# Adding the decay terms of the early attention pairs on TensorE instead of fetching them as tiles

## The chip, the cores and the metric

One core of a Trainium2 chip runs the whole program once. The metric is device microseconds (us) of one execution: 717.03 us, the median of three runs (717.02 to 718.77).

## What is computed

Causal attention with a decay, then two expert layers, all in float32 (cut from the reference):

```python
# q, k, v: (2, 8, 576, 64); s: (2, 8, 576)
scores = q @ k.T / 8
cum = cumsum(maximum(s, 0))
scores = where(causal, -1e9, scores + minimum(-(cum[i] - cum[j]), 0))
attn = softmax(scores); out = attn @ v                 # -> x: (1152, 512)
x = sum_e p[e] * (maximum(x @ w1[e], 0) @ w2[e])       # 4 experts, F = 1024
y = (silu(x @ w_gate) * (x @ w_val)) @ w_out           # F = 1536
```

Softmax does not see a term that is the same along a row, so the kernel adds only the running sums of the keys ("decays") to the scores, a row vector that is the same for all queries of a head.

## The kernel before

**Attention.** Heads are taken in pairs (two heads of 64 dimensions share the 128 partitions). `pairs` (L349) lists sixteen: eight "early" ones for queries 0 to 255 (`pi < EXACT`), then eight "late" ones for queries 256 to 575. For each early pair and each of its two lanes (heads), `group` (L506) makes two score blocks, 128 x 128 and 128 x 256: `scores` (L519) multiplies keys and queries in float32 (L527) and adds a triangular mask by two small fp32r matmuls per block (`tri` times `idr`, L530). `least` (L532) on DVE adds the decays and finds the row extreme (L544, a tensor_tensor_reduce written as a custom instruction and a read of its accumulator). ACT takes the exponential and its sum (`exp`, L553), DVE inverts the sum (`guard`, L559 and L560), ACT or POOL scales the row (`norm`: L335 on ACT, L337 on POOL), PE transposes (`turn`, L598), ACT or DVE copies (`copy`, L327 on ACT, L329 on DVE), and PE multiplies by the values (`products`, L657). `values` splits the result into a high and a low fp32r part, `xh` and `xl`.

**The decays before.** `scan` and `center` turn `s` (16 rows) into `sums`. Each pair needs its two rows spread over all 128 partitions. For pairs 0 and 1 (`NSEL`) PE does it by a one-column selection (`pick`, L461) and ACT copies the result to a `dqe` tile. For pairs 2 to 7 `sums` is written to DRAM (`rows_e`) and fetched six times as a broadcast `dqe` tile, 256 KB each (the last `fetch` of `prepare`). Queries and keys of four pairs are fetched ahead (`NKQ`), the others when an earlier pair is under way.

**The experts.** `into` (L992 to L994, tile `wah`, plain) and `seven` (L1092 to L1094, tiles `wah`/`wsh`, a seven-product form of 2 x 2 blocks) make the hidden rows `hh` and `hl`, `outof` (L1154 to L1156) multiplies back into `acc`. Every product is three fp32r matmuls. Weights come as `raw` tiles (512 KB) and are split into high and low parts by POOL (L331, L340) during attention. Plain units of the first 512 tokens fill PE during attention; how many there are depends on when the plan sees attention end.

**What sets the order.** Every instruction stream is written by `Plan`: tasks have an engine, a cost from a table, a rank and dependencies; `step` takes the task that can start earliest by the plan's own clock, and the lower rank of two. The plan's clock decides the order only; on the chip each engine and each DMA queue runs its stream in order and waits on semaphores. While PE would be idle by the plan's clock, `fill` puts in transposes of the identity (`keep_on`, L409).

Of the kernel before, what the change touches and what calls it, by code (L numbers as in the profile page):

```python
# [17 lines left out]
P = 128  # L18
# [5 lines left out]
NS = 5  # L24
NKQ = 4
NKP = 2
NBE = 3
NBL = 2
NSEL = 2
# [40 lines left out]
CUM2 = 10  # L70
CUMAT = 14.0
FIX2 = 8
HOLDW = 8.0
# [14 lines left out]
    "scale": {"v": (0.063, 0.00104), "a": (0.1, 0.00084), "p": (0.243, 0.00084)},  # L88
# [6 lines left out]
def f32(ap):  # L95
    return ap.bitcast(F32)
# [42 lines left out]
class Task:  # L139
# [141 lines left out]
def attention_moe_swiglu(ctx, tc, q_early, q_late, k, v, s, dp, w1, w2, wg, wv, wo, out):  # L281
# [69 lines left out]
    def attention(ap, ps):  # L351
        BH = B * H
        one = ap.tile([P, S], F32, name="one", tag="ns", bufs=NS)[:BH, :]
        sr = ap.tile([P, NB - 1, 320], F32, name="sr", tag="p", bufs=NPT).rearrange("p c t -> p (c t)")[:BH, :S]
        ncum = ap.tile([P, S], F32, name="ncum", bufs=1)[:BH]
        sums = ap.tile([P, S], F32, name="sums", bufs=1)[:BH]
        early, later, whole = slice(0, 2 * P), slice(2 * P, S), slice(0, S)
        rows_e, rows_l = (scratch.tile([BH, n], F32, name=f"rows{n}", bufs=1) for n in (2 * P, S))
# [3 lines left out]
        mask = ap.tile([P, P], F32, name="mask", bufs=1)  # L362
# [7 lines left out]
        t_sr = fetch(lambda: sr, s, 36, [], -100, take=[ring("p", NPT)])  # L370
# [3 lines left out]
        def upper():  # L374
            nc.gpsimd.memset(mask, 0.0)
            nc.gpsimd.affine_select(
                out=mask, in_=mask, pattern=[[-1, P]], compare_op=ALU.is_ge, fill=-2.0 ** 103, base=0, channel_multiplier=1)
        t_up = add("pool", 0.6, upper, [t_id], rank=-98)
        lo, hi = half
        t_clear = [any_of("v", "fill", 2 * P, lambda e: nc.vector.memset(f32(idr).rearrange("p o n -> p (o n)"), 0.0), [], rank=-97),  # L380
                   any_of("v", "fill", D, lambda e: nc.vector.memset(f32(tri[hi, hi]), -2.0 ** 103), [], rank=-97)]
        spread = [(idr[lo, 0, :], ident[lo, :]), (idr[hi, 0, lo], ident[hi, hi]), (idr[lo, 1, hi], ident[lo, lo]), (idr[hi, 1, :], ident[hi, :])]
        spread2 = [(tri[lo, 0:P], mask[lo, :]), (tri[hi, lo], mask[hi, hi]), (tri[lo, P:], mask[lo, lo]), (tri[hi, P:], mask[hi, hi])]
        t_mask = [any_of("av", "copy", P, lambda e, x=x: move(e, *x), t_clear + [t], rank=-96.5)
                  for y, t in ((spread, t_id), (spread2, t_up)) for x in y]

# [11 lines left out]
        t_scan = add("dve", dve(2 * P), lambda: scan(early), [t, t_one], rank=-98)  # L398
        t_early = add("dve", dve(2 * P), lambda: center(early, P - 1), [t_scan], rank=-98)
        t_rows = [fetch(lambda: rows_e, sums[:, early], 16, [t_early], -97.5)]  # L400
        t = any_of("p", "fill", S - 2 * P, lambda e: positive(e, later), [t_sr], rank=CUM2)
        t_scan2 = add("dve", dve(S - 2 * P), lambda: scan(later), [t, t_scan], give=[(t_sr, ring("p")), (t_one, ring("ns"))], rank=CUM2)

# [11 lines left out]
        def load(quad, deps):  # L415
# [8 lines left out]
            t = fetch(to, v[b, hp // 2, :, :kb], kb * 128, deps, -50 + 10 * quad if quad < 2 else starts[2 * quad] - LOADS,  # L424
# [6 lines left out]
        def prepare(pi, release):  # L431
# [15 lines left out]
            if not exact and pi == EXACT:  # L447
                t_mid = add("dve", dve(S), lambda: center(whole, 3 * P + P // 4 - 1), [t_scan2, t_early] + t_rows, rank=CUM2)
                t_rows.append(fetch(lambda: rows_l, sums, 36, [t_mid], CUM2))
            w = 2 * P if exact else BANK  # L450

            def bias():
                decay[pi] = ap.tile([P, 2, w], F32, name="d" + tag, tag="d" + tag, bufs=NBE if exact else NBL)
                return decay[pi]
            rg = ring("d" + tag, NBE if exact else NBL)
            if pi < NSEL:
                def pick():
                    bias()
                    tp = ps.tile([P, BANK], F32, name="tp", tag="tp", bufs=2)
                    for j in range(2):  # L460
                        nc.tensor.matmul(tp[:, j * w:j * w + w], ident[:BH, BP * j + m:BP * j + m + 1].to_broadcast([BH, P]),  # L461
                                         sums[:, early], start=True, stop=True)
                    decay[pi, "tp"] = tp
                first = add("pe", 2 * pe32(w), pick, [t_early, t_id, chain_d.get(tag)], mode="s", take=[rg, ring("tp")], rank=rank)
                tb = [any_of("a", "bank", 2 * w, lambda e: move(e, decay[pi].rearrange("p j n -> p (j n)"), decay[pi, "tp"]), [first],
                             give=[(first, ring("tp"))], rank=rank - 60)]
            else:
                of = rows_e if exact else rows_l
                first = fetch(bias, lambda: of[m::BP, :w].partition_broadcast(P), 2 * w // 2, [release, t_rows[-1], chain_d.get(tag)], rank + 0.2, take=[rg])
                tb = [first]  # L470
            chain_d[tag] = first
            used[pi] = [(tq, ring(tag)), (first, rg)]
            if not exact:
                def both(j):
                    def to():
                        if j == 0:
# [1111 lines left out]
```

## Time and profile before

| | |
|---|---|
| median of 3 runs | 717.03 us |
| the profiled execution: its own time / its span | 719.07 us / 717.2 us |
| PE, matmul busy | 698.9 us, 97% |
| DVE / ACT / POOL busy | 557.2 / 358.2 / 463.2 us |
| first dense matmul (L992) | 35.97 us |
| last product of attention (L657) starts | 132.06 us |

The profile is of one execution. A matmul's row is longer than the time until the next matmul starts, since they are pipelined; the distance of two starts is what one costs in a row of them. "Idle before <-" at the end of a row is how long the engine stood still before it and what the profile thinks ended the wait. L numbers are lines of the kernel before.

### The profile page before, as it was taken

To read this page: it belongs to the slowest core of one execution; us is meant where nothing else is said; L and a number is where in the kernel's file an instruction comes from. 1 tells how busy PE (TensorE), PEld (TensorE's weight loads), DVE (VectorE), ACT (ScalarE), POOL (GpSimd) and SP (SyncE) were. 2 spreads that over 40 slices of the span, in tenths; PEclk is the share of its full clock that TensorE was granted. 3 is DMA by queue.
4 is the path that set the end of the run, shared out by engine and by line. 5 is a ranking of instruction groups with operands and counts; after the bars stand their busy time and mean duration, and the time that the engine had idled before them with its cause. 6 is when DMAs were issued, how large, how long until landed. Compare 5 with 4: busy or idle time off the path is not lost.

```text
span 717.2 us, 11928 instructions
## 1 busy us (share of the span) xinstructions
PE 698.9 (97%) x4280; PEld 607.2 (85%) x4280; DVE 557.2 (78%) x1081; ACT 358.2 (50%) x757; POOL 463.2 (65%) x436
## 2 busy tenths in 40 slices
PE   8899999999999999999999999999999999999997
PEld 6676666787898989898989888997989999999996
DVE  5686575797278899999999999766884777787665
ACT  5787777423444545555565654655644424233210
POOL 3743242599366667666767678799899868585321
PEclk9999999999999999999999999999999999999999
DMA  8794642112204445465446553222121202010003
GB/s 206 241 306 125 205 135 85 31 58 71 106 0 148 147 157 168 147 207 166 147 160 194 188 186 103 65 86 89 39 80 31 82 23 74 30 31 1 1 1 133
DMA packets 31452, 79.80 MB, mean 111 GB/s; under 512 B 3568, under 2 KB 9216, under 8 KB 31392
## 3 DMA queue, kind: packets, MB, share of 16 engines
q1 hardware_dynamic: 31248, 78.90, 34.4%
q8 instruction: 34, 0.56, 0.3%
q14 instruction: 26, 0.21, 0.1%
q10 hardware_dynamic: 144, 0.13, 0.1%
HBM read 67.16 MB, written 11.85 MB: 110 GB/s over the span
## 4 chain that ended last, share of the span: by engine, by line
PE 74%; DVE 12%; POOL 5%; issue 4%; ACT 4%; DMA 0%; DVEq 0%; ACTq 0%; POOLq 0%
PE h L1092 10%; PE h L1094 10%; PE h L1093 10%; PE o L1154 10%; PE o L1155 10%; PE o L1156 10%; PE tp L598 2%; PE po L657 2%; PE sp L527 2%; DVE tt L1031 1%; ACT ns L553 1%; PE h L992 1%; DVE cc L1111 1%; PE h L994 1%; PE h L993 1%
## 5 line engine op out<-in xcount | busy, mean ns | idle before, releaser
L1111 DVE TENSOR_TENSOR cc<-cc,h 128x320 f32<-128x320 f32 (+1 forms) x282 | 124.9, 452 | 49.3 <-PE h L1094 43.0
L1154 PE MATMUL o<-woh,hh 128*128 128x512 f32 x396 | 157.3, 397 | 2.9 <-DVE acc_a L1242 1.6
L1156 PE MATMUL o<-woh,hl 128*128 128x512 f32 x396 | 154.7, 391 | 1.7 <-DVE hl L340 1.7
L1155 PE MATMUL o<-wol,hh 128*128 128x512 f32 x396 | 155.8, 393 | 0.0
L1092 PE MATMUL h<-xh,wsh 128*128 128x320 f32 (+1 forms) x312 | 92.9, 298 | 0.0
L1094 PE MATMUL h<-xh,wsl 128*128 128x320 f32 (+1 forms) x312 | 92.8, 297 | 0.0
L1093 PE MATMUL h<-xl,wsh 128*128 128x320 f32 (+1 forms) x312 | 92.7, 297 | 0.0
L340 POOL TENSOR_TENSOR wal<-raw,wah 128x512 fp32r<-128x512 f32 (+1 forms) x58 | 70.8, 1230 | 32.4 <-ACT wah L327 31.4
L1156 PEld LDWEIGHTS o<-woh,hl 128*128 128x128 f32 x396 | 74.4, 188 | 18.6 <-DVE hl L340 2.1
L340 POOL TENSOR_TENSOR wol<-raw,woh 128x512 fp32r<-128x512 f32 x54 | 79.2, 1475 | 15.0 <-ACT woh L327 14.5
L1154 PEld LDWEIGHTS o<-woh,hh 128*128 128x128 f32 x396 | 74.5, 188 | 16.6 <-DVE acc_a L1242 2.3
L1155 PEld LDWEIGHTS o<-wol,hh 128*128 128x128 f32 x396 | 74.5, 188 | 10.8
L1211 ACT ACTIVATE cc<-cc 128x640 f32<-128x640 f32 (+1 forms) x46 | 32.1, 698 | 91.7 <-DVE cc L1111 91.6
L340 POOL TENSOR_TENSOR hl<-cc,hh 128x512 fp32r<-128x512 f32 (+1 forms) x28 | 41.9, 1498 | 52.8 <-ACT hh L1214 52.6
L1092 PE MATMUL h<-xh,wah 128*128 128x320 f32 (+1 forms) x234 | 69.4, 297 | 0.0
L1094 PE MATMUL h<-xh,wal 128*128 128x320 f32 (+1 forms) x234 | 69.4, 296 | 0.0
L1093 PE MATMUL h<-xl,wah 128*128 128x320 f32 (+1 forms) x234 | 69.3, 296 | 0.0
L340 POOL TENSOR_TENSOR wsl<-sf,wsh 128x512 fp32r<-128x512 f32 x44 | 66.8, 1537 | 0.8 <-ACT wsh L327 0.8
L1242 DVE SCALAR_TENSOR_TENSOR acc_b<-o,pr,acc_b 128x512 f32<-128x512 f32 x75 | 55.5, 743 | 8.4 <-PE o L1156 8.1
L1092 PEld LDWEIGHTS h<-xh,wsh 128*128 128x128 f32 x312 | 58.9, 189 | 1.5
L1093 PEld LDWEIGHTS h<-xl,wsh 128*128 128x128 f32 x312 | 59.0, 189 | 1.4
L1094 PEld LDWEIGHTS h<-xh,wsl 128*128 128x128 f32 x312 | 59.0, 189 | 0.0
(146 smaller groups left out, 1667.8 us busy)
## 6 DMA issues: line engine op xcount, KB each, us to landing
raw<-in_w SPq DMA_DIRECT2D x42, 512.0 KB, 5.0
n<-hl SPq DMA_DIRECT2D x36, 256.0 KB, 2.3
raw<-n SPq DMA_DIRECT2D x18, 512.0 KB, 3.3
hh<-in_wg SPq DMA_DIRECT2D x12, 512.0 KB, 4.2
hh<-in_wv SPq DMA_DIRECT2D x12, 512.0 KB, 4.0
hh<-in_wo SPq DMA_DIRECT2D x12, 512.0 KB, 3.9
dql<-rows SPq DMA_DIRECT2D x8, 512.0 KB, 5.1
vr<-in_v SPq DMA_DIRECT2D x4, 640.0 KB, 4.4
```

The costliest lines, as they stand in the source:

```text
L340: {"v": nc.vector, "p": nc.gpsimd}[e].tensor_tensor(to, x, f32(y), op=ALU.subtract)
L527: nc.tensor.matmul(sp[j][:, at:at + w], Q[half[j], x], K[half[j], :w], start=True, stop=False)
L598: nc.tensor.transpose(tp[:kn, x * P:x * P + P], box["ns"][lane][:, at + c * P:at + c * P + kn], ident)
L1092: nc.tensor.matmul(hp, wh, h, start=c == 0, stop=False)
L1093: nc.tensor.matmul(hp, wh, l, start=False, stop=False)
L1094: nc.tensor.matmul(hp, wl, h, start=False, stop=c == 1)
L1111: nc.vector.tensor_tensor(part(k), part(x), banks[i], op=ALU.add)
L1154: nc.tensor.matmul(op, hh[:, f, ts], wh[:, f, :], start=f == 0, stop=False)
L1155: nc.tensor.matmul(op, hh[:, f, ts], wl[:, f, :], start=False, stop=False)
L1156: nc.tensor.matmul(op, hl[:, f, ts], wh[:, f, :], start=False, stop=f == NF - 1)
L1211: nc.scalar.activation(src()[:, o], src()[:, o], AF.Relu)
L1242: nc.vector.scalar_tensor_tensor(acc(t), bank_(), sc, acc(t), op0=ALU.mult, op1=ALU.add)
```

## The change

The decays of all early pairs are added on PE. `sums` is split into a high part `sh` and the negative of what is left, `sb` (two DVE instructions, `split`). The sixteen rows of `s` are laid out by the host in four blocks of 32 partitions, so that each half of 64 partitions holds high and low parts of every head; `sel` is a one-hot column with a minus sign. `decays` adds `sel` times `sb` into the open accumulation of the score bank: four fp32r matmuls of 64 rows per pair. The mask becomes a constant second operand of `least`, 128 x 256, instead of eight `tri` matmuls per pair. `pick`, the `dqe` tiles, `rows_e` and its fetches fall away for the early pairs. Queries and keys of all eight early pairs are fetched at once (`NKQ` 8), the first 256 columns of `s` ahead of the other 320. Plan: first weight load not before 16 instead of 8 (`HOLDW`), some costs and ranks are other numbers, a link on the same engine costs nothing. Late pairs keep their `tri` matmuls and fetched decays.

```diff
-NKQ = 4
+NKQ = 8
-CUM2 = 10
+CUM2 = 18
-HOLDW = 8.0
+HOLDW = 16.0
-    "scale": {"v": (0.063, 0.00104), "a": (0.1, 0.00084), "p": (0.243, 0.00084)},
+    "scale": {"v": (0.063, 0.00104), "a": (0.19, 0.00084), "p": (0.243, 0.00084)},
...
-                d.end + (LINK[d.eng] if d.eng != "pe" or e != "pe" else 0.0) if d.eng != "dma" or e != "dma" else 0.0))
+                d.end + (LINK[d.eng] if d.eng != e else 0.0) if d.eng != "dma" or e != "dma" else 0.0))
...
-        t_sr = fetch(lambda: sr, s, 36, [], -100, take=[ring("p", NPT)])
+        t_sr = fetch(lambda: sr[:, early], s[:, early], 128, [], -100, take=[ring("p", NPT)])
+        t_sr2 = fetch(lambda: sr[:, later], s[:, later], 160, [t_sr], -56)
...
+        t = add("dve", 0.22, lambda: nc.vector.reduce_sum(one_hot, ident.rearrange("p (q i) -> p i q", i=32), axis=AX.X), [t_id], rank=-98)
+        t_sel = add("dve", 0.12, lambda: nc.vector.tensor_scalar(sel, one_hot, -1.0, 1.0, op0=ALU.mult, op1=ALU.mult), [t], rank=-98)
...
-        t_rows = [fetch(lambda: rows_e, sums[:, early], 16, [t_early], -97.5)]
+        def split():
+            nc.vector.tensor_copy(sh, sums[:, early])
+            nc.vector.scalar_tensor_tensor(sb, f32(sh), low_rows[:, 0:1], sums[:, early], op0=ALU.mult, op1=ALU.subtract)
+        t_early = add("dve", 0.75, split, [t, t_low], rank=-98)
...
+            if exact:
+                used[pi] = [(tq, ring(tag))]
+                t_ready[pi] = [tk, tq, t_early, t_sel], [t_up]
+                return
...
+                if pi < EXACT:
+                    for qb, at, w in segs:
+                        for j in range(2):
+                            nc.tensor.matmul(sp[j][:, at:at + w], Q[half[j], qb * P:qb * P + P], K[half[j], :w], start=not at, stop=False, skip_group_check=True)
+                    if pi:
+                        decays()
+                    return
...
+            def decays():
+                for qb, at, w in segs:
+                    for j in range(2):
+                        nc.tensor.matmul(box["sp"][j][:, at:at + w], sel[half[j], BP * j + m:BP * j + m + 1].to_broadcast([D, P]), sb[half[j], :w],
+                                         start=False, stop=True, skip_group_check=True)
...
-                        todo = [(at, at + w, box["sp"][lane][:, at:at + w], decay[pi][:, lane, :w])]
+                        todo = [(at, at + w, box["sp"][lane][:, at:at + w], mask[:, 2 * P - w:] if pi < EXACT else decay[pi][:, lane, :w])]
```

What it moves, in the order of the streams. PE, at the first two pairs (`o<-ident` are fillers, `sp` and `h` the score banks, `tp<-sums` the selection). Before:

```order
L409 MATMUL o<-ident 128x128 x18
L527 MATMUL sp<-k_106,qe 128x128 x2
L530 MATMUL sp<-tri,idr 128x128 x2
L530 MATMUL sp<-tri,idr 128x64 x2
L527 MATMUL sp<-k_106,qe 128x256 x2
L530 MATMUL sp<-tri,idr 128x128 x2
L530 MATMUL sp<-tri,idr 128x64 x2
L461 MATMUL tp<-sums,ident 128x256 x4
L527 MATMUL h<-k_107,qe 128x128 x2
```

With the change:

```order
L425 MATMUL o<-ident 128x128 x18
L533 MATMUL sp<-k_109,qe 128x128 x2
L533 MATMUL sp<-k_109,qe 128x256 x2
L425 MATMUL o<-ident 128x128 x3
L548 MATMUL sp<-sb,sel 128x128 x2
L548 MATMUL sp<-sb,sel 128x256 x2
L533 MATMUL h<-k_110,qe 128x128 x2
```

Eight mask matmuls and the selection (for two pairs at once) have gone, four decay matmuls stand in each pair.

SP, the DMA queue, from the fourth transfer on (`dqe` and `rows_104` are the decays, `raw` the weights, `vr` values). Before:

```order
L368 DMA rows_104<-sums 16x256
L368 DMA qe<-in_q_early 128x256
L368 DMA vr<-in_v 128x512 x2
L368 DMA k_110<-in_k 128x256
L368 DMA dqe<-rows_104 128x2x256
L368 DMA rows_105<-sums 16x576
L368 DMA k_111<-in_k 128x256
L795 DMA raw<-in_w 128x1024
L368 DMA dqe<-rows_104 128x2x256
L368 DMA qe<-in_q_early 128x256
L795 DMA raw<-in_w 128x1024
```

With the change, the rows from the last queries on:

```order
L369 DMA k_116<-in_k 128x256
L369 DMA qe<-in_q_early 128x256
L369 DMA rows<-sums 16x576
L369 DMA vr<-in_v 128x512
L818 DMA raw<-in_w 128x1024 x3
L369 DMA vr<-in_v 128x512
L369 DMA k_109<-in_k 128x320
```

All early queries and keys are now ahead of the first weights, no `dqe` transfer is left, and the weights stand behind a `vr` load that waits for the second pair's products to free its buffer.

POOL, from its first scaling (`ns`) on; `wah`/`wal` and `woh`/`wol` are the split weights. Before:

```order
L337 TENSOR_SCALAR ns<-ns,st 128x256
L337 TENSOR_SCALAR ns<-ns,st 128x128
L337 TENSOR_SCALAR ns<-ns,st 128x256 x2
L331 TENSOR_SCALAR wah<-raw 128x512
L337 TENSOR_SCALAR ns<-ns,st 128x128
L340 TENSOR_TENSOR wal<-raw,wah 128x512
```

With the change:

```order
L335 TENSOR_SCALAR ns<-ns,st 128x256 x2
L335 TENSOR_SCALAR ns<-ns,st 128x128 x2
L335 TENSOR_SCALAR ns<-ns,st 128x256
L329 TENSOR_SCALAR wah<-raw 128x512
L338 TENSOR_TENSOR wal<-raw,wah 128x512
L329 TENSOR_SCALAR wah<-raw 128x512
L335 TENSOR_SCALAR ns<-ns,st 128x128
L338 TENSOR_TENSOR wal<-raw,wah 128x512
```

Fourteen scalings now stand ahead of the first weight instead of four (only the last five are shown), and in the whole program POOL has eleven scalings of 128 x 128 instead of three, ACT five instead of thirteen. In the whole program there are also 35 fillers instead of 50, and one plain unit of 512 tokens (24 matmuls of 512 columns) is done in the seven-product form (42 of 256 columns), with one reload of a pair of weight tiles less.

## Rows read from the trace of the kernel before

**Rows 1.** Busy time by stretch: length, PE, PEld, DVE, ACT, POOL; clock, DMA share, GB/s.

```profile
9.37:35.97 26.60, 22.31 (x212) 17.74 (x209) 17.58 (x91) 21.29 (x80) 17.27 (x25) 1.00 0.84 233
62.33:134.40 72.07, 71.10 (x461) 47.19 (x460) 45.56 (x151) 51.18 (x123) 20.81 (x28) 1.00 0.39 125
400.00:500.00 100.00, 97.45 (x556) 86.91 (x555) 81.85 (x128) 56.46 (x107) 80.12 (x72) 1.00 0.38 124
500.00:600.00 100.00, 97.41 (x629) 90.99 (x630) 72.22 (x132) 42.95 (x89) 85.64 (x83) 1.00 0.17 54
```

**Rows 2.** Timeline, PE: dense matmuls of 256 and of 512 columns.

```profile
35.97 0.36 PE L992 MATMUL h<-xh,wah 128*128 128x256 f32 x1
36.17 0.28 PE L993 MATMUL h<-xl,wah 128*128 128x256 f32 x1
36.29 0.28 PE L994 MATMUL h<-xh,wal 128*128 128x256 f32 x1
...
73.94 0.39 PE L993 MATMUL h<-xl,wah 128*128 128x512 f32 x1
74.17 0.40 PE L994 MATMUL h<-xh,wal 128*128 128x512 f32 x1
```

**Rows 3.** Timeline, PE: fillers, first score group, selection.

```profile
1.65 3.79 PE L409 MATMUL o<-ident 128*128 128x128 f32 x18 [1.65 <-POOL ident masks.py:199]
5.37 0.49 PE L527 MATMUL sp<-k,qe 64*128 64x128 f32 x4
...
6.59 1.99 PE L461 MATMUL tp<-sums,ident 16*128 16x256 f32 x8
```

**Rows 4.** Timeline, DVE and ACT: running sums, first decays added, first exponential.

```profile
2.85 0.28 DVE L388 TENSOR_SCALAR sr<-sr 16x256 f32<-16x256 f32 x1 [0.30 <-DMA sr<-in_s]
...
4.34 0.86 DVE L391 TENSOR_TENSOR_SCAN ncum<-one,ncum,sr 16x320 f32<-16x320 f32 x1
...
9.06 0.27 DVE L544 CUSTOM_DVE_ANT_0 ns<-sp,dqe 128x128 f32<-128x128 f32 x1
...
9.37 0.40 ACT L553 ACTIVATE ns<-ns,st 128x128 f32<-128x128 f32 x1 [0.17 <-DVE st L544]
```

**Rows 5.** Timeline, ACT: three scalings and the idle time before them.

```profile
14.84 0.40 ACT L335 ACTIVATE ns<-ns,st 128x128 f32<-128x128 f32 x1 [1.14 <-DVE st L560]
...
20.19 0.40 ACT L335 ACTIVATE ns<-ns,st 128x128 f32<-128x128 f32 x1 [0.88 <-DVE st L560]
...
23.97 0.40 ACT L335 ACTIVATE ns<-ns,st 128x128 f32<-128x128 f32 x1 [1.73 <-DVE st L560]
```

**Rows 6.** Timeline, DVE and SP: decays added, and one issue of a decay transfer.

```profile
13.77 0.58 SPq L368 DMA_DIRECT2D dqe<-rows  x1
...
13.82 0.29 DVE L544 CUSTOM_DVE_ANT_0 ns<-sp,dqe 128x128 f32<-128x128 f32 x1 [1.34 <-PE h L527]
...
17.95 0.29 DVE L544 CUSTOM_DVE_ANT_0 ns<-h,dqe 128x128 f32<-128x128 f32 x1 [1.19 <-DMA dqe<-rows]
...
22.29 0.29 DVE L544 CUSTOM_DVE_ANT_0 ns<-sp,dqe 128x128 f32<-128x128 f32 x1 [2.19 <-POOL wal L340]
```

**Rows 7.** Groups by line and shape, ACT and POOL, 9.3 to 36 us.

```profile
L327 ACT COPY p<-tp 128x384 f32<-128x384 f32 x9 | 4.2, 461 | 0.2 <-PE tp L598 0.2
L335 ACT ACTIVATE ns<-ns,st 128x128 f32<-128x128 f32 x10 | 4.0, 401 | 5.1 <-DVE st L560 5.0
L335 ACT ACTIVATE ns<-ns,st 128x256 f32<-128x256 f32 x4 | 2.0, 504 | 0.0
...
L337 POOL TENSOR_SCALAR ns<-ns,st 128x128 f32<-128x128 f32 x3 | 1.1, 373 | 2.3 <-DVE st L560 1.3 <-ACT ns L553 1.0
```

**Rows 8.** DMA issues of the whole run: count, KB each, median us to landing.

```profile
raw<-in_w SPq DMA_DIRECT2D x42, 512.0 KB, 5.0
```

**Rows 9.** Timeline, POOL and DVE: a weight's low part beside a guard.

```profile
24.52 1.27 POOL L340 TENSOR_TENSOR wol<-raw,woh 128x512 fp32r<-128x512 f32 x1
...
24.89 0.92 DVE L559 TENSOR_SCALAR st<-st 128x2 f32<-128x2 f32 x1 [0.43 <-ACT ns L553]
```

More of the change, by code (lines that the diff above doesn't have):

```diff
@@ L24 @@
 NS = 5
-NKQ = 4
+NKQ = 8
 NKP = 2
-NBE = 3
 NBL = 2
-NSEL = 2
 NPT = 4
@@ L452, in bias @@
+            if pi == EXACT:
+                t_mid = add("dve", dve(S), lambda: center(whole, 3 * P + P // 4 - 1), [t_scan2, t_early], rank=CUM2)
+                t_rows.append(fetch(lambda: rows_l, sums[:BH], 36, [t_mid], CUM2))
             def bias():
-                decay[pi] = ap.tile([P, 2, w], F32, name="d" + tag, tag="d" + tag, bufs=NBE if exact else NBL)
+                decay[pi] = ap.tile([P, 2, BANK], F32, name="dql", tag="dql", bufs=NBL)
                 return decay[pi]
-            rg = ring("d" + tag, NBE if exact else NBL)
@@ L456, in prepare @@
[L456 to L470, printed above, removed]
+            rg = ring("dql", NBL)
@@ L471, in prepare, with both, to @@
+            first = fetch(bias, lambda: rows_l[m::BP, :BANK].partition_broadcast(P), BANK, [release, t_rows[-1], chain_d.get(tag)], rank + 0.2, take=[rg])
+            tb = [first]
             chain_d[tag] = first
             used[pi] = [(tq, ring(tag)), (first, rg)]
[L473 to L476, printed above, removed]
-                            decay[pi, 2] = ap.tile([P, S], F32, name="d2", tag="d2", bufs=NBL)
-                        return decay[pi, 2][half[j]]
-                    return to
-                t2 = []
-                for j in range(2):
-                    t2.append(fetch(both(j), lambda j=j: rows_l[BP * j + m, :].partition_broadcast(D), 144, [release, t_rows[-1]] + t2,
-                                    rank + 0.3, take=[] if j else [ring("d2", NBL)]))
-                def tail(on):
-                    y = decay[pi, 2][:, 4 * P:]
-                    {"v": nc.vector, "p": nc.gpsimd}[on].tensor_tensor(y, y, f32(tri[:, P:]), op=ALU.add)
-                tb.append(any_of("vp", "two", D, tail, t2 + t_mask, rank=rank + 1))
-                used[pi].append((t2[0], ring("d2")))
+            def both(j):
+                def to():
+                    if j == 0:
+                        decay[pi, 2] = ap.tile([P, S], F32, name="d2", tag="d2", bufs=NBL)
+                    return decay[pi, 2][half[j]]
+                return to
@@ new lines, in prepare, with tail @@
+            t2 = []
+            for j in range(2):
+                t2.append(fetch(both(j), lambda j=j: rows_l[BP * j + m, :].partition_broadcast(D), 144, [release, t_rows[-1]] + t2,
+                                rank + 0.3, take=[] if j else [ring("d2", NBL)]))
+            def tail(on):
+                y = decay[pi, 2][:, 4 * P:]
+                {"v": nc.vector, "p": nc.gpsimd}[on].tensor_tensor(y, y, f32(tri[:, P:]), op=ALU.add)
+            tb.append(any_of("vp", "two", D, tail, t2 + t_mask, rank=rank + 1))
@@ L569, in group @@
             ready, bias = t_ready[pi]
-            cost = sum(pe32(w) for _, _, w in segs) + (0.1 if two else 0.13 * len(segs))
-            tS = inorder("s", add("pe", cost, scores, ready + [before.get("s")], mode="f" if two else "s", take=[rg] * 2, rank=i + RANK["s"]))
+            cost = sum(pe32(w) for _, _, w in segs) + (0.4 if pi < EXACT else 0.1 if two else 0.27)
+            if not pi:
+                cost = cost / 2
+                ready = [add("pe", cost, scores, ready[:2], mode="s", take=[rg] * 2, rank=-5), *ready[2:]]
+                used[pi].append((ready[0], rg))
+            tS = inorder("s", add("pe", cost, scores if pi else decays, ready + [before.get("s")], mode="f" if two else "s", take=[rg] * 2 if pi else [], rank=i + RANK["s"]))
             exps, owner = [], {}
@@ L583, in group @@
                 c = min(2, L - x0)
-                tG = inorder("g", add("dve", 0.21, guard(x0, c), exps[x0:x0 + c] + [before.get("g")], rank=i + x0 + RANK["g"]))
+                tG = inorder("g", add("dve", 0.29, guard(x0, c), exps[x0:x0 + c] + [before.get("g")], rank=i + x0 + RANK["g"]))
                 for x, lane, (qb, at, w) in todo[x0:x0 + c]:
```

51 lines of the change are left out of this document (31 added, 20 removed).

## Prediction

> **What bounds the kernel now.** I read the granted clock and the busy time by stretch first, then PE's timeline, then ACT's and DVE's in the stretch where PE is not full, then the streams of both programs.
>
> The clock is 1.00 in every stretch, the upper level of 2.4 GHz, so no difference is explained by it. From 62.33 to 134.40 us PE is busy 71.10 of 72.07 us [rows 1]: late attention has dense matmuls as filling, and PE sets the pace. After attention PE stays near full; what the eye finds missing is 2.55 us between 400 and 500 and 2.59 us between 500 and 600 [rows 1]. So what starts the dense work earlier reaches the end nearly whole, unless something after it gets worse. The first dense matmul starts at 35.97 us [rows 2].
>
> Before it PE is not the limit. From the first exponential at 9.37 us [rows 4] to 35.97 us ACT works 21.29 of 26.60 us, PE 22.31 (with fillers), DVE 17.58 and POOL 17.27 [rows 1]. ACT is the fullest of those whose work is all real, and it stands idle for 5.3 us. Three waits make up 1.14 + 0.88 + 1.73 = 3.75 us of that [rows 5]. Each ends with a guard on DVE, and each guard came late because DVE stood still shortly before: 1.34, 1.19 and 2.19 us [rows 6]. The second names the decay transfer. The first names a matmul and the third a POOL instruction. I read both as decays too: the transfer issued at 13.77 us is the one that the step at 22.29 us needs, 8.5 us later, and by the order the steps at 13.82 and 17.95 us also begin a pair whose decays are fetched. For the third the POOL instruction may be the true cause; no split of a weight stands that early in the changed order, so it would go either way.
>
> **The change, part by part.**
>
> *First exponential.* PE's fillers end before the first scores at 5.37 us as now [rows 3]. Keys and queries of pair 0 are still the first transfers but one. Scores and masks of a pair took 6.59 - 5.37 = 1.22 us [rows 3]. The decays have as many columns as the masks had (2 x 128 + 2 x 256 against 4 x 128 + 4 x 64), of the same 64 rows and type, so I take 1.22 us for scores with decays as well; no row shows a decay matmul, and the bounds are nothing extra (0.6) and twice the masks (1.8). Three fillers lie between, 3.79 / 18 = 0.21 us each [rows 3]. DVE starts at 5.37 + 1.22 + 0.63, about 7.3 us, ACT 0.31 us later [rows 4], 7.6 us instead of 9.37: **1.8 us** earlier. The selection, its two copies on ACT and the wait for them are gone; that is where it comes from. The sums must be there at about 6.6 us: from 2.85 us, up to 0.7 us later for the small constants now ahead on DVE, 1.49 us to the end of the centering [rows 4], and the two instructions of the split at 0.28 (the scaling of 256) to 0.86 us (the scan) each [rows 4] give 4.9 to 6.8 us. It fits, with the upper end 0.2 us late.
>
> *ACT's work to the first dense matmul.* In the changed order ACT has up to there 4 scalings of 128 columns instead of 10, 6 of 256 instead of 4, and 10 copies instead of 9: -6 x 0.401 + 2 x 0.504 + 0.461 [rows 7] = **-0.9 us**. POOL takes the others, in time in which it waits for guards today.
>
> *The decay transfers.* Six of 256 KB and one write go, 1.5 MB, some 6.5 us of the transfers at 233 GB/s [rows 1]. With them go the three waits: **-3.75 us**. What is late next is ACT itself: I leave it the other 1.55 us of idle time. Adding the constant mask costs DVE what adding a fetched tile cost, since the instruction is the same.
>
> *Transfers brought forward.* All early keys and queries, two value tiles and the rows of `s` (now 288 KB) are some 2.9 MB, 12 us at that rate, ready ahead of each pair's need (a pair takes 3 us and 256 KB). One is critical: the second part of `s` lies behind 1.8 MB and lands at about 10 us; POOL scales it, and DVE's scan of it (0.86 us [rows 4]) stands in DVE's order ahead of the next guard. That is a new wait of up to 1.6 us on DVE. ACT then has eight exponentials of at least 0.40 [rows 4] and two scalings of 0.504 [rows 7] queued, to 11.8 us or later, which covers most of it. I take 0 and keep 1.6 as the end.
>
> *Weights.* The first three tiles are now issued behind a value tile that waits for the second pair's products, by my pace at about 16 us. They land 5.0 us later [rows 8], 21 to 22 us; two low parts of 1.27 us [rows 9] and two high parts of at most that make 26 to 27 us. The dense work at 29.5 us is covered by 2 us or more.
>
> The sum to the first dense matmul: 1.8 + 0.9 + 3.75 = 6.45 us, so 29.5 us.
>
> *Dense work.* 24 matmuls of 512 columns at 0.23 us go and 42 of 256 at 0.12 us come [rows 2]: **-0.5 us** on PE. The masks of the early pairs and 15 fillers are in the part that ACT bounds.
>
> *What comes later for it.* Seven low parts of weights run on POOL before 35.97 us today; in the changed order two or three run before the first dense matmul, and the rest fall among the first late pairs. One such part held a guard from 24.89 us until POOL was done at 25.79 us [rows 9]. I add one such hold, **+0.7 us**.
>
> In all -6.45 - 0.5 + 0.7 = -6.25 us. The profiled execution took 719.07 us (span 717.2), so 712.8 us for its like. The median of the runs is 717.03 us, 2.04 us under that execution; I give the forecast on the median: **710.8 us**. A measurement of this kernel can tell about 0.3% from no change, 2.2 us, so "same" is 714.9 to 719.2 us.
>
> The ends of this case: with decays at nothing extra, the whole 5.3 us of idle gone and no hold, 717.0 - 2.4 - 0.9 - 5.3 - 0.5 = 707.9 us. With the scan in full and decays at their upper bound, 710.8 + 1.6 + 0.6 = 713.0 us, and 714 us with a second hold.
>
> **The rivals.**
>
> *POOL holds DVE (0.13).* Eight scalings of 128 columns move to POOL, of 373 ns each [rows 7], into the stretch in which DVE has its guards. If each holds a guard for its whole length and ACT waits for it, 8 x 0.373 = 3.0 us come back: 713.8 us. For it: the guard of [rows 9] did wait for the end of a POOL instruction. Against it: DVE has 9 of 26.6 us free there. The Trainium skill (SBUF — State Buffer, "Who interferes with whom") says that VectorE and GpSimd share a pair of ports as an exclusive lock, held for the whole instruction, and that whoever starts first blocks the other fully. By that rule the trace agrees: the guard ended at 25.81 us, 0.02 us after POOL.
>
> *Given back among the first late pairs (0.12).* Five low parts that now run after the dense work has begun, each with a hold of 0.92 us [rows 9], make 4.6 us where I took 0.7: 714.7 us, and 715.5 us with the scan's wait. PE would then wait for transposes. For it: POOL's order has them back to back. Against it: from 62.33 us on DVE is busy 45.56 of 72.07 us only [rows 1], so that a hold seldom reaches PE.
>
> *The clock falls (0.05), slower than before.* PE has 15 fillers less. If the granted clock went to the lower level (1.2 GHz) before the dense work, PE's work there would double: 22.31 us [rows 1] less 15 x 0.21 = 19.2 us, 38.3 us from 7.2 us on, the first dense matmul at 45.5 instead of 29.5 us and the end at 727 us. It decides from the point at which the slack (29.5 - 7.2 - 19.2 = 3.1 us), the gain of 6.25 us and 2.2 us are used up: 11.5 of the 19.2 us at the lower level. For it: the very first fillers took 0.21 us each for 128 columns, dense matmuls 0.12 us for 256. Against it: 1.00 in all rows, with PE idle 4.3 us in this stretch already.
>
> *The later plan is better too (0.07).* New costs re-set the order to the end. If the 5.1 us of idle at 400 to 600 us went as well: 705.7 us. Nothing in the rows says so; it could as well grow by some.
>
> That the change doesn't do what it says has no room: the order shows no `dqe` transfer and four decay matmuls in each early pair.
>
> **How the numbers follow.** My case has 0.63 (707.9 to 714), held ports 0.13, the better plan 0.07: faster 0.83. Given back is mostly within 0.3%: same 0.12. The clock: slower 0.05. The range 705 to 715 us takes in the first two cases and most of the better plan, and leaves out the clock, the worse half of the third and a little at both ends.
>
> **What the changed profile would show.** Right: first exponential near 7.6 us, no wait on ACT over 1 us before the dense work, first plain dense matmul of 256 columns at 28.5 to 31 us, last product of attention some 8 us earlier than 132 us, the stretches after it unchanged. Wrong: a DVE wait near 10 us with ACT idle behind it (the scan); guards of 0.5 us or more beside POOL's scalings; PE waits between 30 and 60 us; a granted clock under 1.00; or a first dense matmul at 30 us with the end hardly moved, which would say that PE's row of dense work has slack that the busy time hides.

## The result, and the profile after

The changed kernel takes **708.03 us** (median of four runs, 707.28 to 708.60) against 717.9 us of the kernel before beside it (717.02 to 720.47): ratio 0.9855, 95% interval 0.9838 to 0.9873. The profiled execution took 707.56 us, its span is 705.8 us, 11.4 us under the span of 717.2 us that the forecast was summed against.

The first exponential, the scan of the second part of `s` and the first dense matmuls (timeline of the changed kernel; start, duration, instruction, idle time before it):

```profile
7.79 0.40 ACT L572 ACTIVATE ns<-ns,st 128x128 f32<-128x128 f32 x1 [4.14 <-DVE st L563]
...
11.64 0.88 DVE L403 TENSOR_TENSOR_SCAN ncum<-one,ncum,sr 128x320 f32<-128x320 f32 x1 [1.32 <-POOL sr L400]
...
29.21 0.37 PE L1015 MATMUL h<-xh,wah 128*128 128x256 f32 x1
```

The exponential is 1.58 us earlier than in [rows 4], the first dense matmul 6.76 us earlier than in [rows 2]. Busy time by stretch (length, PE, PEld, DVE, ACT, POOL; clock, DMA share, GB/s), the first line between those two events:

```profile
7.79:29.21 21.42, 18.68 (x170) 13.94 (x167) 16.89 (x92) 20.09 (x77) 13.23 (x23) 1.00 0.61 191
400.00:500.00 100.00, 98.36 (x582) 88.27 (x582) 81.05 (x135) 56.66 (x113) 75.80 (x74) 1.00 0.33 107
500.00:600.00 100.00, 98.39 (x637) 91.97 (x637) 75.50 (x133) 41.38 (x82) 83.84 (x74) 1.00 0.17 53
```

ACT stands idle for 1.33 us of 21.42, against 5.31 of 26.60 in [rows 1], and none of its waits behind a guard is longer than 0.24 us. PE's missing time at 400 to 600 us went from 5.14 to 3.25 us. What PE waited for after the last attention product, before (from 135 us) and after (from 123 us; releaser, total, times, longest):

```profile
PE o L1156 <- DVE hl L340: 1.7, 1, 1.7
PE o L1154 <- DVE acc_a L1242: 1.6, 2, 1.3
PE o L1270 <- DVE xl L1281: 1.5, 1, 1.5
PE h L1092 <- DVE cc L1111: 1.0, 1, 1.0
```

```profile
PE o L1177 <- DVE acc_a L1265: 1.6, 1, 1.6
PE o L1177 <- DVE xl L1304: 1.1, 1, 1.1
PE h L1115 <- DVE cc L1134: 0.9, 2, 0.5
PE h L1115 <- ACT cc L325: 0.7, 1, 0.7
```

With the smaller ones 6.4 us became 4.8.

To compare orders that put different dense work into attention I take the dense work out: the matmuls that the order has in a stretch, at 0.12 us for 256 columns in, 0.143 for 320 and 0.23 for 512, close to the spacing of their starts (0.119, 0.147 and 0.231 us). "Net" is what is left, in us (with it what a dense matmul costs above this price, as the first one behind a matmul of attention does): up to the first late scores (384 columns), from there to the end of the last product, and after it. At these prices every kernel has 587.6 to 588.3 us of dense work.

| profiled execution | span | first exp. | net to late scores | net late attention | net after |
|---|---|---|---|---|---|
| before | 717.2 | 9.37 | 38.5 | 70.9 | 19.6 |
| changed | 705.8 | 7.79 | 31.0 | 69.3 | 17.9 |
| e1 plan alone | 723.5 | 12.00 | 43.1 | 68.9 | 23.2 |
| e2 old numbers | 709.4 | 8.33 | 33.9 | 69.7 | 17.5 |
| e3 select all | 727.2 | 9.36 | 51.6 | 69.4 | 17.8 |
| e4 ACT longer | 707.3 | 8.81 | 32.1 | 69.6 | 17.9 |
| e5 no fillers | 708.9 | 6.95 | 31.2 | 72.1 | 18.0 |
| e6 late fillers out | 705.7 | 7.87 | 30.6 | 69.5 | 18.0 |
| e7 select all, fed | 719.5 | 10.49 | 44.3 | 67.6 | 19.3 |
| e8 DVE longer | 706.4 | 7.86 | 31.5 | 69.4 | 17.9 |
| e9 weights early | 707.7 | 7.85 | 33.0 | 69.1 | 17.2 |
| e10 decays ahead | 718.4 | 10.13 | 37.3 | 71.8 | 21.1 |
| e11 scan fed | 704.0 | 8.03 | 30.5 | 68.1 | 17.8 |
| e12 weights late | 709.8 | 7.88 | 30.4 | 68.8 | 22.4 |

So the 11.4 us are 7.5 up to the late scores, 1.6 in late attention, 1.7 after it, and 0.5 of dense work, to 0.1 us. Where the clock falls in part of an execution, the timed runs of one kernel lie apart (e7: 719.7 to 737.5 us); there the ratio is of the fast runs alone, and I go by the profile.

### The profile page after: what moved, and what is told of

Same layout as the page of the kernel before. It is cut to its first block, busy times and chain, and to the rows that moved or that the text cites. A ratio compares the mean times of both kernels' runs of the same rounds, so it can differ in the third digit from the quotient of the medians.

```text
span 705.8 us, 11848 instructions
## 1 busy us (share of the span) xinstructions
PE 690.4 (98%) x4243; PEld 602.6 (85%) x4243; DVE 547.2 (78%) x1091; ACT 357.1 (51%) x753; POOL 452.0 (64%) x437
## 4 chain that ended last, share of the span: by engine, by line
PE 85%; DVE 6%; POOL 3%; ACT 2%; DMA 2%; issue 1%; SPq 0%; ACTq 0%; POOLq 0%; DVEq 0%
PE o L1177 12%; PE h L1115 12%; PE o L1178 12%; PE h L1117 12%; PE h L1116 12%; PE o L1179 12%; PE po L680 3%; PE tp L621 3%; PE sp L540 2%; DVE tt L1054 2%; PE h L1015 2%; PE h L1017 1%; PE h L1016 1%; DVE xl L338 1%; DMA dps<-in_dp 1%
## 5 line engine op out<-in xcount | busy, mean ns | idle before, releaser
L1134 DVE TENSOR_TENSOR cc<-cc,h 128x320 f32<-128x320 f32 (+1 forms) x288 | 128.7, 453 | 53.8 <-PE h L1117 43.6
L1115 PE MATMUL h<-xh,wsh 128*128 128x320 f32 (+1 forms) x320 | 95.3, 298 | 0.7 <-ACT cc L325 0.7
L1117 PE MATMUL h<-xh,wsl 128*128 128x320 f32 (+1 forms) x320 | 95.1, 297 | 0.0
L1116 PE MATMUL h<-xl,wsh 128*128 128x320 f32 (+1 forms) x320 | 95.0, 297 | 0.0
L338 POOL TENSOR_TENSOR hl<-cc,hh 128x512 fp32r<-128x512 f32 (+1 forms) x30 | 45.1, 1504 | 75.0 <-ACT hh L1237 75.0
L338 POOL TENSOR_TENSOR wol<-raw,woh 128x512 fp32r<-128x512 f32 x52 | 74.0, 1438 | 10.1 <-ACT woh L325 9.3
L1115 PE MATMUL h<-xh,wah 128*128 128x256 f32 (+1 forms) x240 | 71.2, 297 | 0.5 <-DVE cc L1134 0.5
L1117 PE MATMUL h<-xh,wal 128*128 128x256 f32 (+1 forms) x240 | 71.1, 296 | 0.0
L1116 PE MATMUL h<-xl,wah 128*128 128x256 f32 (+1 forms) x240 | 71.0, 296 | 0.0
L338 POOL TENSOR_TENSOR wsl<-sf,wsh 128x512 fp32r<-128x512 f32 x44 | 63.1, 1454 | 2.2 <-ACT wsh L325 2.2
```

The costliest lines, as they stand in the source:

```text
L338: {"v": nc.vector, "p": nc.gpsimd}[e].tensor_tensor(to, x, f32(y), op=ALU.subtract)
L1115: nc.tensor.matmul(hp, wh, h, start=c == 0, stop=False)
L1116: nc.tensor.matmul(hp, wh, l, start=False, stop=False)
L1117: nc.tensor.matmul(hp, wl, h, start=False, stop=c == 1)
L1134: nc.vector.tensor_tensor(part(k), part(x), banks[i], op=ALU.add)
```

## The experiments

**Decays or plan numbers?** The change does two things: the decays become matmuls, and the plan gets other numbers. e1 gives the kernel before the numbers alone (the edit is cut here; it also takes the new cost of the scores), e2 takes them from the changed kernel.

```diff
 e1, on the kernel before
-"a": (0.1, 0.00084), "p": (0.243       +"a": (0.19, 0.00084), "p": (0.243
-if d.eng != "pe" or e != "pe" else     +if d.eng != e else
-add("dve", 0.21, guard                 +add("dve", 0.29, guard
-CUM2 = 10; HOLDW = 8.0                 +CUM2 = 18; HOLDW = 16.0
 e2, on the changed kernel: the same lines back, and the old cost of the scores
```

> The kernel before with the change's plan numbers only (cost of ACT's scaling and of the guard, no hand-over time within an engine, weights held to 16 us, later rank of the second scan); decays still selected and fetched as before. Theory A (the start was gained by the decays, the rest by the new order after it): first exponential at 9.4 us as in the kernel before, at least two ACT waits of 0.8 us or more ahead of the first dense matmul, which starts at 34 to 37 us; the end 713 to 717 us. Theory B (the plan numbers made the gain): first dense matmul before 32 us and the end at 707 to 711 us.

Measured: 723.21 us, ratio 1.0072 (1.005 to 1.0094), slower than either theory allowed. Net to the late scores it is 4.6 us behind the kernel before, in two parts. At the first exponential it is 2.6 us late (12.00 us): the new order puts the selection ahead of the first scores, and it takes 3.78 us where it took 1.99 in [rows 3] (PE's timeline of e1):

```profile
5.47 3.78 PE L461 MATMUL tp<-sums,ident 16*128 16x256 f32 x8
9.18 0.80 PE L527 MATMUL sp<-k,qe 64*128 64x128 f32 x4
```

The rest is lost from 25 to 40 us (busy time by stretch of e1):

```profile
25.00:30.00 5.00, 3.32 (x37) 2.35 (x31) 3.42 (x17) 3.85 (x14) 0.37 (x1) 1.00 1.02 295
30.00:35.00 5.00, 3.35 (x20) 2.62 (x22) 2.56 (x6) 0.80 (x2) 4.16 (x5) 0.57 1.01 352
35.00:40.00 5.00, 5.00 (x39) 4.28 (x37) 3.57 (x15) 3.38 (x13) 3.12 (x6) 0.75 0.98 279
```

and POOL's longest wait there:

```profile
POOL wah L331 <- DMA raw<-in_w: 4.6, 1, 4.6
```

The weights, now requested at 25.8 us among the decay and value transfers, held POOL for 4.6 us, a scaling waited in POOL's queue behind them, PE stood still for 3.3 us for it, and the granted clock was at the lower level of 1.2 GHz (0.50) from 31 to 37 us. The numbers alone are a loss on the kernel before.

> The changed kernel with the plan numbers of the kernel before; decays on PE, queries and keys at once as changed. Theory A: first exponential at 7.6 to 7.9 us, first late scores (384 columns) at 31 to 35 us instead of 39.9, the end 708 to 713 us. Theory B (plan numbers): first late scores at 37 us or later, the end 714 to 718 us.

Measured: 711.83 us, ratio 0.9909 (0.9895 to 0.9924): theory A. First late scores at 36.7 us; its upper end was 35, but 1.4 us more dense work lies ahead of them. The decays with the old numbers give 4.6 of the 7.5 us of the start; the numbers give 2.9 on top. ACT's waits behind guards up to the late scores show the same: 5.5 us in the kernel before, 2.8 in e2, 0.2 in the changed kernel. e2 holds the early fetch of all queries and keys together with the decay matmuls, and no run separates the two. The fetch has a part: in the kernel before scores start at 18.22 us, after PE has been idle for 0.73 us and 0.1 us after their queries have landed.

**What did the numbers give?** In e2 the DVE guards are long again (groups by line: busy, mean ns; guards up to the first late scores in the kernel before, the changed kernel, e2 and e9):

```profile
L559 DVE TENSOR_SCALAR st<-st 128x2 f32<-128x2 f32 x14 | 4.5, 319 | 2.0 <-ACT ns L553 2.0
```

```profile
L578 DVE TENSOR_SCALAR st<-st 128x2 f32<-128x2 f32 x14 | 2.8, 203 | 0.1
```

```profile
L578 DVE TENSOR_SCALAR st<-st 128x2 f32<-128x2 f32 x14 | 7.0, 501 | 1.8 <-ACT ns L572 1.4
```

```profile
L578 DVE TENSOR_SCALAR st<-st 128x2 f32<-128x2 f32 x16 | 5.5, 345 | 1.2 <-ACT ns L572 0.7
```

POOL has 8, 4, 8 and 7 low parts of weights in these stretches, 1.28 us each. e9 sets back the one number that puts them there:

```diff
-HOLDW = 16.0
+HOLDW = 8.0
```

> The changed kernel with one number of the plan set back: weights may be fetched from 8 us instead of 16 us of the planned time on. Among the early pairs up to the first late scores POOL then has more splits of weights. Theory P (POOL's low parts of 1.28 us hold the DVE guards, and what the plan numbers gave is mostly this): 6 to 8 low parts there instead of 4, the 14 guards at a mean of 0.40 us or more instead of 0.20, first late scores net of dense work at 32.5 to 34.5 us instead of 31.0, the end 709.5 to 712. Rival (it was the share of scalings on ACT, 21 in the run with the old numbers, 11 in the changed kernel): net 30.5 to 31.5, the end 707 to 709.

Measured: 709.85 us, ratio 0.989 (0.9871 to 0.9908); net 33.0. Theory P: 7 low parts, and 2.0 of the 2.9 us. ACT has 12 scalings there, against 11 in the changed kernel and 21 in e2, so the rival falls. The guards' mean of 0.345 us is under the 0.40 I gave, so holds of guards are not all of it.

How a guard is held is seen in the changed kernel (timelines, DVE, then POOL):

```profile
24.94 0.64 DVE L578 TENSOR_SCALAR st<-st 128x2 f32<-128x2 f32 x1
26.28 0.23 DVE L578 TENSOR_SCALAR st<-st 128x2 f32<-128x2 f32 x1
40.34 1.25 DVE L578 TENSOR_SCALAR st<-st 128x2 f32<-128x2 f32 x1
```

```profile
11.70 1.04 POOL L335 TENSOR_SCALAR ns<-ns,st 128x128 f32<-128x128 f32 x1
...
24.27 1.28 POOL L338 TENSOR_TENSOR wal<-raw,wah 128x512 fp32r<-128x512 f32 x1
26.12 0.37 POOL L335 TENSOR_SCALAR ns<-ns,st 128x128 f32<-128x128 f32 x1
40.26 1.29 POOL L338 TENSOR_TENSOR wol<-raw,woh 128x512 fp32r<-128x512 f32 x1
```

A guard alone takes 0.17 us. Each of these three ends 0.02 to 0.04 us after POOL's instruction, and the second of them waits for a scaling, not for a low part. So scalings hold a guard too, only shorter: they take 0.37 to 0.48 us, a high part 0.62, a low part 1.28. In e9 the longest of ACT's waits behind a guard (1.06 us, at 31.34 us) follows a guard that a low part held for 1.15 us. That the 2.0 us are these holds alone is not shown: e9 also moves the weights' transfers ahead of others.

**Were the three waits decay transfers?** The trace of the kernel before says when the transfers landed. Issues, then the time from issue to landing of the transfers issued at 6.85, 10.56 and 13.77 us ([rows 6] has the third issue):

```profile
6.85 0.38 SPq L368 DMA_DIRECT2D dqe<-rows  x1
10.56 0.38 SPq L368 DMA_DIRECT2D dqe<-rows  x1
```

```profile
DMA to landing us min/median/max: 6.8/6.8/6.8
DMA to landing us min/median/max: 7.3/7.3/7.3
DMA to landing us min/median/max: 8.4/8.4/8.4
```

They landed at about 13.7, 17.8 and 22.1 us, and the three late steps of [rows 6] start at 13.82, 17.95 and 22.29 us, 0.1 to 0.2 us later. All three waits were for decays, also the two for which the profile names PE and POOL.

Two other ways to have the decays early, without matmuls of scores and decays in one bank: e3 selects all of them on PE and copies them on ACT (e7 is e3 with filler transposes against the fall of the clock), e10 fetches them ahead.

```diff
 e3                    e7: e3, and                            e10
-NSEL = 2             +    for _ in range(4): keep_on()      -NKQ = 4; NBE = 3
+NSEL = 8             +BUSY = 0.80                           +NKQ = 8; NBE = 6
```

> The kernel before, with the decays of all eight early pairs selected by PE and copied by ACT as those of the first two are, so that no early decay is fetched; each of six pairs has one more ACT copy of 512 columns (0.59 us in the kernel before), 3.5 us in all. Theory A (the three waits of 3.75 us are decay transfers, and ACT bounds): the waits go, the copies take their place, first late scores at 38 to 41 us, the end within 2 us of the kernel before. Rival (the waits have another cause): they stay, first late scores at 43 us or later and the end at 720 us or more. Rival (ACT does not bound): the waits go and the copies lie in idle time, first late scores before 37 us.

Measured: 728.8 us, ratio 1.014 (1.0122 to 1.0159). It tests nothing of what it was for, since the clock fell (busy time by stretch):

```profile
5.00:10.00 5.00, 4.31 (x32) 3.39 (x30) 1.56 (x9) 1.67 (x4) 0.00 (x0) 1.00 0.69 205
10.00:15.00 5.00, 5.00 (x36) 3.73 (x34) 2.00 (x14) 3.63 (x12) 1.55 (x3) 0.68 0.90 284
15.00:20.00 5.00, 5.00 (x29) 3.92 (x28) 1.93 (x13) 2.18 (x8) 1.75 (x2) 0.50 0.63 221
```

It stays at 0.50 to 45 us. Before the fall PE did selections of 16 rows, and waited 0.69 us between them.

> The kernel before with all early decays selected by PE and copied by ACT, as in the earlier run with that edit, and four filler transposes behind each of the 16 selections (and more of the planned ones), so that the clock stays up. It removes the early decay transfers without the decay matmuls of the change. Theory A1 (the three waits were decay transfers): granted clock 1.00, no ACT wait over 0.9 us behind a guard, net of dense work first late scores at 34 to 37 us (38.5 in the kernel before: 3.75 us of waits less 3.5 us of copies that partly fall into idle time), the end 713 to 718. Rival (the waits have another cause): such waits stay, 39 us or later and an end above 719.

Measured: 731.02 us, ratio 1.0057 (1.0018 to 1.0095). In the profiled execution the clock holds (1.00), but the first exponential comes at 10.49 us, three waits behind guards (2.0 us, the longest 1.11) stay up to the first dense matmul at 39.14 us, and net 44.3 is worse than both theories: the selections take 9.0 us of PE instead of 2.0, and the fillers behind them and six copies of 0.59 us come on top. Inconclusive on the waits.

> The kernel before with tiles for all eight early queries and six early decays instead of four and three, so that all of them are fetched ahead of the weights and of the third value tile; decays still fetched and added by DVE. Theory A1 (the three ACT waits of 3.75 us were decays fetched late): no ACT wait of 0.8 us or more behind a guard after the first exponential, which stays at 9.4 us; first late scores net of dense work at 34.0 to 36.0 us instead of 38.5, the end 713 to 716. Rival (other causes, such as POOL's splits behind the guards, and the transfers only took the blame): net 37.5 to 39, the end 717 to 719.

Measured: 720.46 us, ratio 1.0021 (0.9996 to 1.0045), above both forecasts. ACT's waits from the first exponential to the first dense matmul (35.97 us in the kernel before, then e10, 35.36 us):

```profile
ACT ns L335 <- DVE st L560: 5.0, 5, 1.7
ACT p L327 <- PE tp L598: 0.2, 1, 0.2
```

```profile
ACT p L327 <- PE tp L598: 3.0, 2, 2.6
ACT ns L335 <- DVE st L560: 1.6, 3, 1.1
```

5.0 us behind guards became 1.6. Theory A1 allowed no such wait of 0.8 us, and one of 1.08 us is left, at 33.82 us. It is no decay: the last of them landed at 20.8 us. The time did not come with it: the granted clock was 0.51 from 10 to 15 us, PE became late (3.0 us of waits for its transposes), the first exponential is 0.76 us later, and net is 37.3, between the two forecasts. How much the waits would give at the full clock stays open.

**Does ACT bound the early pairs?** One instruction more per pair, on ACT (e4) or on DVE (e8); nothing reads its result.

```diff
 e4, behind the last exponential of a pair
+nc.scalar.copy(ap.tile([P, P], F32, name="extra", tag="extra", bufs=1), mask[:, :P])
 e8, behind the last addition of a pair
+nc.vector.memset(ap.tile([P, 2 * P], F32, name="extra", tag="extra", bufs=1), 0.0)
```

> The changed kernel with one more ACT copy of 128 columns behind the last exponential of each early pair (eight copies, whose result nothing reads; order otherwise the same). The row of an ACT copy of 384 columns is 0.45 us, of a scaling of 128 0.40 us at the most, so 8 x 0.3 to 0.4 = 2.4 to 3.2 us of ACT. Theory A (ACT bounds up to the first dense matmul, and what is late there is late at the end): first dense matmul 2.0 to 3.2 us later than 29.2 us, the end 1.8 to 3.5 us above the changed kernel's 708.0. Rival (ACT is full but not the bound, weights or PE's chain are): first dense matmul under 1 us later, the end within 1 us. Rival (later slack takes it up): first dense matmul 2 to 3 us later, the end under 1 us.

> The changed kernel with one more DVE instruction (a memset of 128 x 256, 0.27 us in the kernel's own row) behind the last addition of each early pair, 2.2 us in all; order otherwise the same. The same addition on ACT moved the first dense matmul by 0.13 us beyond its later first exponential. Theory D (DVE's place between scores and exponential, and its guards, set the pace): first exponential to first dense matmul 1.5 us or more longer than 21.4, the end 709.5 to 711. Rival E (no single engine is the bound, the early pairs are a chain with slack on each): under 0.7 us, the end within 1 us of 708.

Measured: e4 708.07 us, ratio 0.986 (0.9845 to 0.9875); e8 708.45 us, 0.9853 (0.9837 to 0.9869). From the first exponential to the first dense matmul (busy time of e4, then of e8):

```profile
8.81:30.36 21.55, 19.40 (x170) 14.43 (x167) 18.08 (x94) 21.12 (x83) 13.61 (x23) 1.00 0.57 187
```

```profile
7.86:29.38 21.52, 19.36 (x170) 14.23 (x167) 19.28 (x97) 20.05 (x76) 13.62 (x23) 1.00 0.61 196
```

Seven of the eight added instructions lie in these stretches, 2.0 us of copies (0.29 us each) and 1.9 us of memsets. They lengthen 21.42 us by 0.13 and 0.10, and neither is seen at the end. In e4 ACT's busy time rose by 1.03 us (the rows of its instructions overlap, and one scaling fewer is in the stretch) and its idle time fell from 1.33 to 0.43. e4's first dense matmul is 1.15 us later than the changed kernel's, between theory A and its rival, but 1.02 of that is there at its first exponential. Theory A of e4 and theory D of e8 fall: ACT is 94% busy in the changed kernel without being the bound, since 1 us more fits in. What less work on ACT would give, no run shows.

**Do the fillers hold the clock?**

```diff
 e5 (e6: the first 18 stay)
-nc.tensor.transpose(idle["p"][:, :P], ident, ident)
+idle["n"] = idle.get("n", 0) + 1
```

> The changed kernel without any of its 35 filler transposes, all other instructions in the same order. Two kernels of this study showed the granted clock at 0.50 for 7 and 34 us of the first 50, so the rival of the clock is not empty. Theory C (the fillers hold the clock, as that rival had it): the granted clock is 0.50 in several of the 5 us stretches up to 40 us, the first pair's scores take about 2 us instead of 0.93, first late scores at 40 us or later instead of 32.4, the end 715 to 728 us. Rival (the work itself is enough): the clock as in the changed kernel from 10 us on, first late scores within 1.5 us of 32.4, the end 707 to 710 us.

> The changed kernel with its first 18 fillers and without the 17 that follow among the early pairs; all other instructions in the same order. Theory C2 (the 17 are what keeps the clock, so the change, which has 15 fillers less than the kernel before, stood near the edge): granted clock under 1.00 in some stretch of 10 to 40 us, the end 712 us or more. Rival (margin is left): 1.00 from 10 us on, the end within 1.5 us of 708.

Measured: e5 707.74 us, ratio 0.9855 (0.9832 to 0.9878); e6 707.63 us, 0.9846 (0.9831 to 0.986). The rival without clock trouble is right in both: a granted clock of 1.00 in every 5 us up to 50 us. e5's profiled execution has one stretch at 0.83 from 50 to 60 us and is its longest run (710.64 us; the other three 707.3 to 707.9). In the median the fillers buy nothing here. Without the first 18 the first scores start when their keys land (PE's timeline of e5):

```profile
4.02 1.65 PE L533 MATMUL sp<-k,qe 64*128 64x128 f32 x8 [4.02 <-DMA k<-in_k]
```

The first exponential is then at 6.95 us, 0.84 us earlier, and the late scores are not.

**The scan, and weights later still.**

```diff
 e11                                        e12: e11, and
-s[:, later], 160, [t_sr], -56)            -HOLDW = 16.0
+s[:, later], 160, [t_sr], -59.55)         +HOLDW = 20.0
```

> The changed kernel with the second part of the rows of s fetched third instead of ninth, so that POOL's scaling of it need not wait for the transfer and DVE's scan not for POOL (1.32 us in the changed kernel, with ACT idle for 0.81 us behind it). Theory S (that wait is on the path): scan wait under 0.3 us, first late scores net of dense work 0.8 to 1.3 us earlier than 31.0, the end 706.5 to 707.3. Rival E (slack takes it up, as it took the 2.2 us of work added to ACT or to DVE): within 0.4 us of 31.0, the end within 0.7 us of 708.

Measured: 705.83 us, ratio 0.9831 (0.9813 to 0.9849). The scan now runs where DVE waits anyway:

```profile
6.51 0.88 DVE L403 TENSOR_TENSOR_SCAN ncum<-one,ncum,sr 128x320 f32<-128x320 f32 x1 [0.59 <-POOL sr L400]
```

Net to the late scores it gives 0.5 us (between the two forecasts), and late attention is 1.2 us shorter in the new order. The time is under both. It is the lowest of the study, 2.2 us below the changed kernel's median; they did not run side by side and their intervals overlap.

> The kernel with the second part of s fetched third (705.8 us), and the weights held back to 20 us of the planned time instead of 16, the opposite of the run with 8. Theory P (POOL's splits of weights among the early pairs hold the guards, the fewer the better): at most 3 low parts before the first late scores, the guards at a mean of 0.25 us or less instead of 0.33, first late scores net of dense work at 29.5 to 30.3 us instead of 30.5, the end 704.5 to 705.8. Rival W (the weights then arrive too late: in the changed kernel the second low part ended 1.5 us before the first dense matmul): PE waits for weights or runs fillers ahead of the first dense matmul, net 31.5 to 34 us, the end 707 to 710.

Measured: 713.63 us, ratio 0.9943 (0.9931 to 0.9955). Neither: net 30.4 is as in e11, and PE did not wait for weights. Up to the first late scores POOL had three low parts, as theory P asked (five up to 35 us), but the guards' mean is 0.316 us and not under 0.25. In e11 it is 0.333 with four low parts, as long as in the kernel before with eight (0.319), and its net of 30.5 is the better one than the changed kernel's 31.0 with 0.203. So the guards' mean does not tell the start: in e11 ACT waits only 0.6 us behind guards, so a long hold need not make it wait. The loss is far behind the place of the edit (PE's waits from 125 us on):

```profile
PE o L1177 <- DVE acc_a L1265: 3.4, 2, 2.4
PE h L1117 <- POOL wsl L338: 1.3, 2, 0.9
```

The plan made another order to the end, and net after attention is 22.4 us instead of 17.8.

## Why the prediction was right, and where not

The time lies in the range, 2.8 us under the forecast. On the profiled executions the sum said -6.25 us and the trace says -11.4.

- **First exponential**, -1.8 us: -1.58. The decays on PE do replace selection, copies and the wait. The missing 0.22 us are the fillers: their 18 take 4.02 us in the changed kernel instead of 3.79, and the first scores start at 5.59 us instead of 5.37. This start varies: the eight score matmuls took 0.93 us in the changed kernel and 1.65 in e4, whose first exponential is at 8.81 us with the same instructions ahead of it.
- **ACT's work**, -0.9 us, and "what is late next is ACT itself": this reasoning failed. ACT's busy time fell by 1.2 us (21.29 to 20.09), but e4 shows that it was no bound: 1 us more of it lengthens the stretch by 0.13.
- **The three waits**, -3.75 us: gone, and ACT's idle time with them, 5.31 to 1.33 us. All three were decay transfers, as read; the landings show it, also for the third, for which POOL was left open.
- **What had no term**: the prediction counted POOL's low parts ahead of the first dense matmul (seven before, two or three after, three by the trace) and gave nothing for those that go. e9 shows that the later weights are worth 2.0 us of the start. So the shift of the first dense matmul (6.45 forecast, 6.76 measured) is right partly by luck: what the ACT term counted came in reality from there.
- **The scan**, taken as 0 with 1.6 as the end: a wait of 1.32 us, with 0.81 us of ACT idle behind it, at the place and for the cause that were named. e11 makes it 0.5 us up to the late scores. Mis-sized, within its bounds.
- **Weights**, covered by 2 us or more: the first one was issued at 18.26 us instead of about 16, and the second low part ended 1.5 us before the first dense matmul. It was enough, by less.
- **Dense work**, -0.5 us: -0.5 by count.
- **Holds among the first late pairs**, +0.7 us: one came, and it cost 0.96 us on PE. The guard at 40.34 us above was held for 1.25 us, and ACT and PE waited behind it (timelines of the changed kernel):

```profile
41.88 1.33 ACT L333 ACTIVATE ns<-ns,st 128x512 f32<-128x512 f32 x2 [1.58 <-DVE st L579]
42.66 0.66 PE L621 MATMUL tp<-ident,ns 128*128 128x128 f32 x4 [0.96 <-ACT ns L333]
```

Late attention became 1.6 us shorter all the same, 2.3 us off the forecast and the largest miss. No wait of PE explains it: its listed waits there went from 2.0 to 2.5 us. By the distances of starts, the dense matmuls in this stretch cost 1.1 us less above their price (3.7 to 2.6 us; they stand in 18 groups between matmuls of attention instead of 22), transposes 0.5 and scores 0.3 less. Why the plan made fewer groups is not shown.
- **The stretches after it unchanged**: 1.7 us less, PE's waits 6.4 to 4.8 us. This was the small rival of the better later plan, sized at 5.1 us. It is no merit of the new numbers: with the old ones (e2) net after is 17.5.

The rivals. *POOL holds DVE*: the mechanism is real, and its size was far too large. In the changed kernel two of the 14 guards up to the late scores were held by a scaling, by 0.03 and 0.07 us, not eight by 0.37: a guard seldom starts while a scaling runs. The rule of the Trainium skill (SBUF — State Buffer, "Who interferes with whom") agrees with these holds. *Given back*: one hold reached PE, as above, not five (and by its own terms that rival's second figure is 716.3 us, not 715.5). *The clock* did not fall ahead of the dense work in the changed kernel, nor without fillers (e5). It fell in three kernels that still select decays (e1, e3, e10), so the mechanism was worth its place; the kernel before, which selects those of two pairs, held 1.00 in its profile, so what makes it fall is not shown.

## What to carry to other kernels

The releaser that a profile names for a wait can be the wrong one: set the start against the landing of every transfer that the instruction needs. A stage where one engine is 94% busy may still have slack: add a known amount of work to it and look at the next stage's start before costing its relief. Where a planner writes the order, judge a change of its numbers by stretches (start, middle, end, net of the common work), since an edit that concerns the first 30 us can cost 4 us behind attention; and look for an off-path engine whose long instructions sit between the short ones of the engine on the path.

## What had not been expected of the hardware

- A guard waits for nearly everything that POOL does: of 156 guards in the 14 traces that start with more than 0.19 us of a POOL instruction left, 147 end 0.02 to 0.03 us after it, low parts, high parts and scalings alike. Two of the other nine started beside POOL's clamp of 320 columns, which did not hold them (e2: 0.20 us at 10.74 us, the clamp runs to 11.75).
- A POOL scaling of 128 columns, 0.37 us alone, took 1.04 us when it started during DVE's scan of 320 columns (11.70 us above, the scan from 11.64 to 12.52): DVE holds POOL as well.
- POOL's clamp and scaling of 320 columns (L400) takes 1.28 us, also with DVE idle; its multiplication of 512 columns (L329) takes 0.62.
- The column of the granted clock reads 1.00 up to 10 us in e5 although the same eight matmuls took 1.65 us there and 0.93 in the changed kernel, so it does not show the low rate at the start. The Trainium skill (TensorE: Matmul & The Clock Gate, Part 1: The HAM clock gate) says that the number of matmuls before the rise differs between runs of one kernel; 7.79, 7.86, 8.81 us for the first exponential behind the same instructions agree.
